# A fused attention and two-layer kernel: batch 0's first keys, second half's masks, their copies and part of a decoding on other engines

## The chip, the core and the metric

The kernel runs on one core of a Trainium2 chip. The metric is the device time of one execution in microseconds. Engines are named as in the profile: PE is TensorE, PEld its weight loads, DVE VectorE, ACT ScalarE, POOL GpSimd, SP SyncE with its DMA queue.

## The reference

Attention with a causal mask and a bias that decays with the positions, then a gated layer, then a second layer; all in fp32.

```python
cum = np.cumsum(np.maximum(s, 0.0), axis=-1)
bias = -(cum[:, :, :, None] - cum[:, :, None, :])
scores = np.where(causal, -1000000000.0, scale * q @ k.T + np.minimum(bias, 0.0))
attn = np.exp(scores - np.max(scores, axis=-1, keepdims=True))
attn = attn / (np.sum(attn, axis=-1, keepdims=True) + 1e-09)
x = attn @ v                       # 4 batches, 8 heads, 576 positions, head size 64
x = (silu(x @ w_gate) * (x @ w_val)) @ w_out      # 2304 x 512, inner size 1536
out = silu(x @ w_in) @ w_out2                     # inner size 2048
```

## The kernel before

Attention goes by batch `b`, head pair `g` and half: half A holds query tiles 0 to 2 (rows 0 to 319), half B tiles 3 and 4 (rows 320 to 575). One such half is a unit; batch 0 has units 0 to 7 (A and B in turn). A unit goes through these functions:

- `masks` (L189): GpSimd writes the row of biases with the causal mask into `e` by `affine_select`. For half A that is the whole row (GATE is 0), for half B only the last 128 columns of each tile; the columns ahead of GATE are read from `c` directly.
- `score_mm` (L203): TensorE makes the scores of both heads side by side, each on 64 rows of the array (the head size is 64).
- `score_min` (L220): VectorE adds scores and biases into `e` and keeps the extreme of each row. Where a piece crosses GATE it is cut in two (one part from `c`, one from `e`).
- `expo` (L240), `inverse` (L250): exponentials and their sums on ScalarE, the inverse of the sums on VectorE.
- `first_keys` (L259) and `normal` (L270): they scale the rows by the inverse. `first_keys` writes the first 64 keys of both heads beside each other into a tile `z` (on ScalarE in half A and in the last unit, on GpSimd else); `normal` scales the other columns in place on GpSimd.
- `turn_mm` (L276): in batch 0 first 8 products of the identity with itself, which nobody reads (fillers); then TensorE transposes 128x128 blocks of `e` and the `z` tiles into PSUM.
- `turned` (L301): copies the two PSUM tiles to `pt`, tile 0 on ScalarE and tile 1 on VectorE.
- `value_mm` (L311): probabilities by values, 64 columns for each head, both side by side; `x_high` and `x_low` split the result into two parts.

For the first 66.5 us (batch 0) all engines run in the order of the code: `first_slot(u)` (L745) issues scores of unit `u`, values of unit `u - 2` and turns of unit `u - 1`; ScalarE's and VectorE's queues have `expo` and `score_min` of `u` ahead of the copies of `u - 1`. Between the slots stand the decoding of weight chunk 0 (`decode`, `unpack` L388: two ScalarE copies out of 64-bit words, then two VectorE operations, in slots 2, 3, 5 and 6) and its cut into two parts (`w_cut`). Behind batch 0 only TensorE's order is written by hand; batches 1 to 3 of the attention are mixed there with the first layer (`gate` L522, `down` L534), and the other engines' order is chosen by a scheduler.

PSUM: batch 0's scores use all four buffers of `ps_m` for each unit, so a unit's scores wait until `score_min` of the unit before has read a bank. Turns and values share two buffers of `ps_a`.

Of the kernel before, what the change touches and what calls it, by code (L numbers as in the profile page):

```python
# [8 lines left out]
F32 = mybir.dt.float32  # L9
F32R = mybir.dt.float32r  # L10
U32 = mybir.dt.uint32
AF = mybir.ActivationFunctionType
ALU = mybir.AluOpType

B, H, S, D = 4, 8, 576, 64
NT, DM = B * S, H * D
F1, F2 = 1536, 2048
P = 128
# [11 lines left out]
TILES = [(0, 64), (64, 128), (192, 128), (320, 128), (448, 128)]  # L30
# [32 lines left out]
QMASK = 1.0e9  # L63
# [3 lines left out]
def kernel(  # L67
# [9 lines left out]
    nc = tc.nc  # L77
# [5 lines left out]
    def pool(name, bufs, space=None, scope=ctx, side="left"):  # L83
        kw = {"space": space} if space is not None else {}
        return scope.enter_context(tc.tile_pool(name=name, bufs=bufs, side=side, reuse_waits="tile", **kw))
# [14 lines left out]
    z_p = pool("z", 4, scope=attention, side="right")  # L100
# [9 lines left out]
    def copy(eng, out, in_, scale=1.0):  # L110
        if eng == "a":
            act_last[:] = [nc.scalar.activation(out=out, in_=in_, func=AF.Copy, scale=scale).ins]  # L112
        elif eng == "v":
            nc.vector.tensor_scalar(out=out, in0=in_, scalar1=scale, scalar2=None, op0=ALU.mult)
        else:
            nc.gpsimd.tensor_scalar(out=out, in0=in_, scalar1=scale, scalar2=1.0, op0=ALU.mult, op1=ALU.mult)


    ident = const.tile([P, P], F32, name="ident")
# [29 lines left out]
    st = {}  # L149
    first_v, first_z = [], []  # L150

    def zeros():
        for n in range(2):
            t = zero_p.tile([P, P], F32, tag=f"v0_{n}", name="vz")
            nc.vector.memset(t, 0.0)
            first_v.append(t)
        first_z.append(zero_p.tile([P, P], F32, tag="z0", name="z0"))
        nc.vector.memset(first_z[0], 0.0)

    def qk_load(b, g):  # L160
        t = qkr_p.tile([P, 2, S], F32, tag="qkr", name="qkr")
        for i in range(2):
            nc.sync.dma_start(out=t[i * D : i * D + D], in_=qk[b, 2 * g + i].rearrange("t d s -> d t s"))
        st[b, g, "qkc"] = (t, None)
# [24 lines left out]
    def masks(b, g, half):  # L189
        c = st[b, g, "qkc"][1]  # L190
        es = st[b, g, half, "e"] = {}
        for i in HALF[half][0]:
            q0, r = TILES[i]
            g0, wd = GATE[i], q0 + r
            e = e_p.tile([P, 2, S], F32, tag="e", name="e")
            for hd in range(2):
                nc.gpsimd.affine_select(
                    out=e[:r, hd, g0:wd], in_=c[:r, hd, g0:wd], pattern=[[-1, wd - g0]], compare_op=ALU.is_ge,
                    fill=-8.0 * QMASK, base=q0 - g0, channel_multiplier=1,
                )  # L200
            es[i] = e

    def score_mm(b, g, half):  # L203
        t = st[b, g, "qkc"][0]
        if b == 0:
            banks = [[ps_m.tile([P, 512], F32, tag="m", name="psc") for _ in range(2)] for _ in range(2)]
        else:
            banks = [ps_a.tile([P, 2, 512], F32, tag="a", name="psc") for _ in range(2)]
            banks = [[p[:, 0], p[:, 1]] for p in banks]
        st[b, g, half, "s"] = banks  # L210
        for i, bank, o, c0, n in PACK[half]:
            q0 = TILES[i][0]
            for hd in range(2):
                d0 = hd * D
                nc.tensor.matmul(  # L215
                    out=banks[bank][hd][:, o : o + n], lhsT=t[d0 : d0 + D, 0, q0 : q0 + P],
                    rhs=t[d0 : d0 + D, 1, c0 : c0 + n], start=True, stop=True,
                )

    def score_min(b, g, half, i):  # L220
        c, e, banks = st[b, g, "qkc"][1], st[b, g, half, "e"][i], st[b, g, half, "s"]
        r, g0 = TILES[i][1], GATE[i]
        m = [None, None]
        for k, bank, o, c0, n in PACK[half]:
            if k != i:
                continue
            for hd in range(2):
                for k0, end, gate in ((c0, min(g0, c0 + n), c), (max(g0, c0), c0 + n, e)):
                    if k0 >= end:
                        continue  # L230
                    m2 = sm_p.tile([P, 1], F32, tag="m", name="m")
                    nc.vector.tensor_tensor_reduce(  # L232
                        out=e[:r, hd, k0:end], in0=banks[bank][hd][:r, o + k0 - c0 : o + end - c0],
                        in1=gate[:r, hd, k0:end], scale=-0.125,
                        scalar=3.0e38 if m[hd] is None else m[hd][:r], op0=ALU.add, op1=ALU.min, accum_out=m2[:r],
                    )
                    m[hd] = m2
        st[b, g, half, "m", i] = m
# [18 lines left out]
        nc.vector.reciprocal(out=rl[:r], in_=l[:r])  # L257

    def first_keys(b, g, half, i):  # L259
        r, e, rl = TILES[i][1], st[b, g, half, "e"][i], st[b, g, half, "l", i]  # L260
        z = first_z[0] if i == 0 else z_p.tile([P, P], F32, tag="z", name="z")
        st[b, g, half, "z", i] = z
        for hd in range(2):
            f = rl[:r, hd : hd + 1]
            if half in ZACT or (b, g) == (0, NP - 1):
                nc.scalar.activation(out=z[:r, hd * D : hd * D + D], in_=e[:r, hd, :D], func=AF.Copy, scale=f)
            else:
                copy("g", z[:r, hd * D : hd * D + D], e[:r, hd, :D], f)

    def normal(b, g, half, i):  # L270
        r, e, rl = TILES[i][1], st[b, g, half, "e"][i], st[b, g, half, "l", i]
        for hd in range(2 if i > 0 else 0):
            x = e[:r, hd, D : sum(TILES[i])]
            copy("g", x, x, rl[:r, hd : hd + 1])

    def turn_mm(b, g, half):  # L276
        tiles, base, n = HALF[half]
        es = st.pop((b, g, half, "e"))
        ps = [ps_a.tile([P, 2, 512], F32, tag="a", name="ptr") for _ in range(2)]
        put = []  # L280
        for _ in range(8 if b == 0 else 0):
            nc.tensor.matmul(out=ps[0][:, 0, :P], lhsT=ident, rhs=ident, start=True, stop=True)
        for j, tile, o in PLACE[half]:
            k0 = TILES[j][0]
            for i in tiles:
                q0, r = TILES[i]
                if q0 < k0:
                    continue
                for hd in range(2):
                    x = o + q0 - max(k0, base)  # L290
                    nc.tensor.transpose(ps[tile][:, hd, x : x + r], es[i][:r, hd, k0 : k0 + P], ident[:r, :r])  # L291
            off = max(k0, base) - base
            put.append((j, tile, o, off, n - off))
        for i, tile, hd, o in PLACE0[half]:
            q0, r = TILES[i]
            z = st.pop((b, g, half, "z", i))
            r = P
            nc.tensor.transpose(ps[tile][:, hd, o : o + r], z[:r], ident[:r, :r])
        st[b, g, half, "p"] = (ps, put, [None, None])

    def turned(b, g, half, k):  # L301
        n = HALF[half][2]
        ps, _, pt = st[b, g, half, "p"]
        pt[k] = pt_p.tile([P, 2, 512], F32, tag="pt", name="pt")
        w = WIDE[half][k]
        if w is None:
            copy("av"[k], pt[k][:, 0, :n], ps[k][:, 0, :n])
        else:
            copy("av"[k], pt[k][:, :, :w], ps[k][:, :, :w])

    def value_mm(b, g, half):  # L311
        tiles, base, n = HALF[half]
# [74 lines left out]

    def unpack(zz, t, k, part="av"):  # L388
        lo, hi = t[:, :, 0], t[:, :, 1]
        if "a" in part:  # L390
            nc.scalar.activation(out=zz, in_=hi.bitcast(F32), func=AF.Copy, scale=2.0**-112)
            nc.scalar.activation(out=k, in_=lo, func=AF.Copy, scale=0.937 * 2.0**-29)
        if "v" in part:
            nc.vector.scalar_tensor_tensor(
                out=k, in0=zz.bitcast(U32), scalar=3, in1=k, op0=ALU.logical_shift_left, op1=ALU.bitwise_or
            )
            nc.vector.scalar_tensor_tensor(
                out=zz.bitcast(U32), in0=hi, scalar=0x80000000, in1=k, op0=ALU.bitwise_and, op1=ALU.bitwise_or
            )
# [345 lines left out]
    def first_slot(u):  # L745
# [37 lines left out]
        if x:  # L783
            if u < H - 1:
                inverse(*x, tiles[-1])
                masks(*units[u + 1])
                first_keys(*x, tiles[-1])
            normal(*x, tiles[-1])
# [10 lines left out]
    def body():  # L799
        everything = ExitStack()  # L800
        everything.enter_context(tc.manual_schedule(engines=None))
        setup()
        zeros()
        qk_load(*pairs[0])
        qk_load(*pairs[1])
# [241 lines left out]
```

## Time and profile before

| what | us |
|---|---|
| median of 3 runs | 1011.53 (1010.31 to 1012.63) |
| span of the profiled execution, first to last instruction (no other time of it is given) | 1010.2 |
| TensorE busy | 999.4 |
| first 66.5 us (batch 0): TensorE busy | 62.68 |
| 66.5 to 105 us: TensorE busy | 36.26 of 38.50 |
| 105 us to the end: TensorE busy | 900.44 of 905.20 |

The profiled execution's span is 1.3 us under the median of the runs. A busy time of TensorE is the time in which a product is in flight; how close the products follow each other is read from the starts of the groups in the timeline.

### The profile page before, as it was taken

How to read it: one execution, taken by the hardware profiler on the slowest of the kernel's cores; microseconds unless marked ns; L12 is line 12 of the kernel's file. 1: busy time of each engine (PE TensorE's matmuls, PEld its weight loads, DVE VectorE, ACT ScalarE, POOL GpSimd, SP SyncE). 2: the span in 40 equal slices, each digit the busy share in tenths (PEclk: the TensorE clock that was granted, in tenths of full speed). 3: DMA queues.
4: the chain of work that ended last, by engine and by line, in shares of the span. 5: the costliest groups of instructions: out<-in, count | busy, mean ns of one | idle time of the engine just before them, and what ended most of it. 6: DMA issues, size and time to landing. Idle time of an engine off the chain costs nothing.

```text
span 1010.2 us, 19666 instructions
## 1 busy us (share of the span) xinstructions
PE 999.4 (99%) x6992; PEld 942.4 (93%) x6992; DVE 565.3 (56%) x1434; ACT 530.0 (52%) x1294; POOL 590.7 (58%) x753
## 2 busy tenths in 40 slices
PE   8999999999999999999999999999999999999998
PEld 6788898899899899988899999999999999999998
DVE  5887847635645645445552323266666566665555
ACT  6878877615665536665542443244544335543333
POOL 4667765613976655756651665455467458674445
PEclk9999999999999999999999999999999999999999
DMA  8688897758797799876668686797767866896662
GB/s 233 160 266 298 268 349 233 258 180 276 244 332 250 254 317 307 284 240 239 254 232 314 243 308 247 287 391 294 263 249 271 321 228 253 292 342 233 243 225 103
DMA packets 81619, 267.19 MB, mean 265 GB/s; under 512 B 9904, under 2 KB 29360, under 8 KB 66160
## 3 DMA queue, kind: packets, MB, share of 16 engines
q1 hardware_dynamic: 81376, 265.73, 75.2%
q8 instruction: 55, 0.90, 0.4%
q14 instruction: 44, 0.36, 0.1%
q10 hardware_dynamic: 144, 0.20, 0.1%
HBM read 208.15 MB, written 57.75 MB: 263 GB/s over the span
## 4 chain that ended last, share of the span: by engine, by line
PE 93%; ACT 2%; DMA 2%; POOL 1%; DVE 1%; issue 1%; SPq 0%; POOLq 0%; DVEq 0%
PE pgv L504 9%; PE pgv L505 9%; PE pgv L506 9%; PE pu L646 6%; PE pu L650 6%; PE pu L649 6%; PE po L691 6%; PE po L692 6%; PE po L693 6%; PE po L504 5%; PE pv L333 5%; PE po L505 5%; PE po L506 5%; PE psc L215 4%; PE ptr L291 3%; DMA r<-in_w_dram 1%
## 5 line engine op out<-in xcount | busy, mean ns | idle before, releaser
L504 PE MATMUL pgv<-xt,wt 128*128 128x288 f32 x768 | 229.5, 299 | 1.2 <-DVE u L515 1.2
L505 PE MATMUL pgv<-xt,wt 128*128 128x288 f32 x768 | 226.3, 295 | 0.1
L506 PE MATMUL pgv<-xt,wt 128*128 128x288 f32 x768 | 226.1, 294 | 0.0
L623 POOL TENSOR_TENSOR h<-u,h 128x384 fp32r<-128x384 f32 x72 | 75.1, 1043 | 142.1 <-ACT h L112 127.9
L504 PEld LDWEIGHTS pgv<-xt,wt 128*128 128x128 f32 x768 | 144.1, 188 | 12.3 <-DVE m L232 6.3
L505 PEld LDWEIGHTS pgv<-xt,wt 128*128 128x128 f32 x768 | 144.1, 188 | 0.3 <-DVE xt L348 0.3
L506 PEld LDWEIGHTS pgv<-xt,wt 128*128 128x128 f32 x768 | 144.0, 188 | 0.0
L112 ACT ACTIVATE h<-u 128x288 fp32r<-128x288 f32 (+1 forms) x168 | 79.8, 475 | 95.4 <-DVE u L516 94.3
L518 POOL TENSOR_TENSOR h<-u,h 128x288 fp32r<-128x288 f32 x96 | 80.0, 836 | 83.1 <-ACT h L112 83.1
L504 PE MATMUL po<-h,wt 128*128 128x288 f32 x384 | 114.8, 299 | 0.0
L505 PE MATMUL po<-h,wt 128*128 128x288 f32 x384 | 113.1, 294 | 0.0
L506 PE MATMUL po<-h,wt 128*128 128x288 f32 x384 | 113.0, 294 | 0.0
L691 PE MATMUL po<-h,wt 128*128 128x384 f32 x336 | 112.4, 335 | 0.0
L692 PE MATMUL po<-h,wt 128*128 128x384 f32 x336 | 112.3, 334 | 0.0
L693 PE MATMUL po<-h,wt 128*128 128x384 f32 x336 | 112.3, 334 | 0.0
L646 PE MATMUL pu<-x,wt 128*128 128x384 f32 x330 | 111.8, 339 | 0.1
L649 PE MATMUL pu<-x,wt 128*128 128x384 f32 x330 | 111.7, 339 | 0.0
L650 PE MATMUL pu<-x,wt 128*128 128x384 f32 x330 | 111.7, 339 | 0.0
L623 POOL TENSOR_TENSOR h<-t,h 128x384 fp32r<-128x384 f32 x96 | 107.2, 1139 | 5.5 <-ACT h L112 5.5
L652 ACT ACTIVATE s<-pu 128x384 f32<-128x384 f32 x48 | 23.6, 492 | 149.6 <-PE pu L650 149.6
L245 ACT ACTIVATE e<-e,m 64x64 f32<-64x64 f32 (+4 forms) x160 | 88.4, 554 | 25.3 <-DVE m L232 24.7
L702 DVE TENSOR_TENSOR acc<-po,acc 128x384 f32<-128x384 f32 x144 | 76.8, 557 | 36.3 <-PE po L693 35.6
(113 smaller groups left out, 2227.8 us busy)
## 6 DMA issues: line engine op xcount, KB each, us to landing
wt<-w_d SPq DMA_DIRECT2D x54, 1024.0 KB, 7.0
wt<-wu_d SPq DMA_DIRECT2D x48, 1024.0 KB, 9.0
wt<-wu_d SPq DMA_DIRECT2D x47, 768.0 KB, 6.5
r<-in_w_dram SPq DMA_DIRECT2D x36, 512.0 KB, 6.7
w_d<-wt SPq DMA_DIRECT2D x18, 1024.0 KB, 8.4
r<-in_w_dram SPq DMA_DIRECT2D x64, 256.0 KB, 7.2
qkr<-in_qk_dram SPq DMA_DIRECT2D x32, 288.0 KB, 8.0
cumb<-cum_d SPq DMA_DIRECT2D x15, 576.0 KB, 9.2
```

Source lines behind the costliest of these rows:

```text
L245: nc.scalar.activation(out=e[:r, hd, :wd], in_=e[:r, hd, :wd], func=AF.Exp, bias=m[hd][:r], scale=-1.0, accum_out=l[:r, hd : hd + 1],)
L504: nc.tensor.matmul(out=ps[:, :n], lhsT=a, rhs=xh, start=(k == 0), stop=False)
L505: nc.tensor.matmul(out=ps[:, :n], lhsT=a, rhs=xl, start=False, stop=False)
L506: nc.tensor.matmul(out=ps[:, :n], lhsT=c, rhs=xh, start=False, stop=(k == last))
L518: engines[LO[ph]].tensor_tensor(out=lo, in0=u, in1=hi.bitcast(F32), op=ALU.subtract)
L623: nc.gpsimd.tensor_tensor(out=h[:, 1], in0=u, in1=h[:, 0].bitcast(F32), op=ALU.subtract)
L646: nc.tensor.matmul(out=o, lhsT=a, rhs=x[:, 0, kk], start=fresh and kk == 0, stop=False, skip_group_check=True)
L649: nc.tensor.matmul(out=o, lhsT=a, rhs=x[:, 1, kk], stop=False, **more)
L650: nc.tensor.matmul(out=o, lhsT=c, rhs=x[:, 0, kk], stop=kk == 1, **more)
L691: nc.tensor.matmul(out=ps, lhsT=a, rhs=h[:, 0], start=fresh, stop=False, skip_group_check=True)
L692: nc.tensor.matmul(out=ps, lhsT=a, rhs=h[:, 1], stop=False, **more)
L693: nc.tensor.matmul(out=ps, lhsT=c, rhs=h[:, 0], stop=e == 1, **more)
```

## The change

All of it acts on batch 0 only, and on the decoding of chunk 0 in slots 2, 3, 5 and 6.

- A tile `tri` is made once: 0 on and under the diagonal, -8e9 above it. In half B `masks` issues nothing; after each pair of score products two products with the identity add the columns of `tri` that fall on the diagonal block to the scores in PSUM. `score_min` then reads the biases from `c` over the whole piece, in one piece.
- `first_keys` issues nothing in batch 0; `normal` scales all columns, also of tile 0. `turn_mm` turns the first 64 keys of each head by a product with the identity into 64 PSUM rows, two products for each tile in place of one transpose of `z`.
- Both `pt` copies of half B are on ScalarE.
- The copy of the high words in `unpack` is on GpSimd where the two parts of the decoding are issued apart (chunk 0); elsewhere it stays on ScalarE.

```diff
+        tri = st["tri"] = z_p.tile([P, P], F32, tag="z", name="tri")
+        nc.gpsimd.affine_select(
+            out=tri, in_=first_z[0], pattern=[[-1, P]], compare_op=ALU.is_ge, fill=-8.0 * QMASK, base=0,
+            channel_multiplier=1,
+        )
...
-            for hd in range(2):
+            for hd in range(0 if b == 0 and half == "B" else 2):
                 nc.gpsimd.affine_select(
...
+            lo, end = max(q0, c0), min(q0 + P, c0 + n)
+            for hd in range(2 if b == 0 and half == "B" else 0):
+                nc.tensor.matmul(
+                    out=banks[bank][hd][:, o + lo - c0 : o + end - c0], lhsT=ident, rhs=st["tri"][:, lo - q0 : end - q0],
+                    start=False, stop=True, skip_group_check=True,
+                )
...
+        if b == 0 and half == "B":
+            g0 = sum(TILES[i])
...
     def first_keys(b, g, half, i):
+        if b == 0:
+            return
...
-        for hd in range(2 if i > 0 else 0):
-            x = e[:r, hd, D : sum(TILES[i])]
+        for hd in range(2 if i > 0 or b == 0 else 0):
+            x = e[:r, hd, D if b > 0 else 0 : sum(TILES[i])]
...
+            if b == 0:
+                for k in range(2):
+                    nc.tensor.matmul(
+                        out=ps[tile][k * D : k * D + D, hd, o : o + r], lhsT=es[i][:r, k, :D], rhs=ident[:r, :r],
+                        start=True, stop=True,
+                    )
+                continue
...
+        eng = "a" if (b, half) == (0, "B") else "av"[k]
...
-            copy("av"[k], pt[k][:, :, :w], ps[k][:, :, :w])
+            copy(eng, pt[k][:, :, :w], ps[k][:, :, :w])
...
+        if part == "a":
+            copy("g", zz, hi.bitcast(F32), 2.0**-112)
+        elif "a" in part:
+            nc.scalar.activation(out=zz, in_=hi.bitcast(F32), func=AF.Copy, scale=2.0**-112)
         if "a" in part:
-            nc.scalar.activation(out=zz, in_=hi.bitcast(F32), func=AF.Copy, scale=2.0**-112)
             nc.scalar.activation(out=k, in_=lo, func=AF.Copy, scale=0.937 * 2.0**-29)
```

TensorE's queue from the scores of unit 1 (half B) to the turns of unit 0, before (`psc` scores, `ptr` turned blocks, `z` first keys; the 128x128 identity products are the fillers):

```order
L215 MATMUL psc<-qkr 128x448 x2
L215 MATMUL psc<-qkr 128x64 x2
L215 MATMUL psc<-qkr 128x512 x2
L282 MATMUL ptr<-ident 128x128 x8
L291 MATMUL ptr<-ident,e 128x128 x6
L298 MATMUL ptr<-ident,z_151 128x128
L298 MATMUL ptr<-ident,z 128x128 x2
```

The same place after the change:

```order
L220 MATMUL psc<-qkr 128x448 x2
L226 MATMUL psc<-tri,ident 128x128 x2
L220 MATMUL psc<-qkr 128x64 x2
L226 MATMUL psc<-tri,ident 128x64 x2
L220 MATMUL psc<-qkr 128x512 x2
L226 MATMUL psc<-tri,ident 128x64 x2
L297 MATMUL ptr<-ident 128x128 x8
L306 MATMUL ptr<-ident,e 128x128 x6
L313 MATMUL ptr<-ident,e 64x64 x2
L313 MATMUL ptr<-ident,e 64x128 x4
```

Six mask products now stand between the score pairs, and six products stand for three transposes; the rest of TensorE's queue is the same in both kernels.

GpSimd's queue from unit 0's last `normal` to the masks of unit 4, before (`e` from `cumb` is a mask, `e` from `e,rl` a `normal`):

```order
L116 TENSOR_SCALAR e<-e,rl 128x256 x2
L116 TENSOR_SCALAR z<-e,rl 128x64 x2
L116 TENSOR_SCALAR e<-e,rl 128x384 x2
L197 AFFINE_SELECT e<-cumb 64x64 x2
L197 AFFINE_SELECT e<-cumb 128x192 x2
L197 AFFINE_SELECT e<-cumb 128x320 x2
L116 TENSOR_SCALAR z<-e,rl 128x64 x2
L116 TENSOR_SCALAR e<-e,rl 128x512 x2
L116 TENSOR_SCALAR e<-e,rl 128x128 x2
L197 AFFINE_SELECT e<-cumb 128x128 x4
L116 TENSOR_SCALAR e<-e,rl 128x256 x2
L116 TENSOR_SCALAR z<-e,rl 128x64 x2
```

The same place after the change:

```order
L116 TENSOR_SCALAR e<-e,rl 128x320 x2
L116 TENSOR_SCALAR e<-e,rl 128x448 x2
L202 AFFINE_SELECT e<-cumb 64x64 x2
L202 AFFINE_SELECT e<-cumb 128x192 x2
L202 AFFINE_SELECT e<-cumb 128x320 x2
L116 TENSOR_SCALAR e<-e,rl 128x576 x2
L116 TENSOR_SCALAR e<-e,rl 64x64 x2
L116 TENSOR_SCALAR e<-e,rl 128x192 x2
L116 TENSOR_SCALAR e<-e,rl 128x320 x2
L116 TENSOR_SCALAR wraw<-r_181 128x512
L116 TENSOR_SCALAR e<-e,rl 128x448 x2
```

The four selects of half B and the `z` products are gone, the `normal` rows are 64 columns wider, and the decode copy of the first quarter of chunk 0 (`wraw`) stands behind unit 2's `normal` and ahead of unit 3's.

ScalarE's queue in slot 2 (half A of unit 2, copies of unit 1), before:

```order
L112 ACTIVATE xt<-pv 128x320
L266 ACTIVATE z_151<-e,rl 64x64 x2
L245 ACTIVATE e,l<-e,m 128x320 x2
L266 ACTIVATE z<-e,rl 128x64 x2
L112 ACTIVATE pt<-ptr 128x1024
L266 ACTIVATE z<-e,rl 128x64 x2
L391 ACTIVATE wraw<-r_177 128x512
L392 ACTIVATE dk<-r_177 128x512
```

The same place after the change:

```order
L112 ACTIVATE xt<-pv 128x320
L258 ACTIVATE e,l<-e,m 128x320 x2
L112 ACTIVATE pt<-ptr 128x1024 x2
L418 ACTIVATE dk<-r_181 128x512
L258 ACTIVATE e,l<-e,m 128x448 x2
```

The `z` products and one decode copy left ScalarE, and the second `pt` copy came. Behind batch 0 the queues of ScalarE, VectorE, GpSimd and SP differ by some swapped rows up to about 100 us of the trace of before, and not behind.

## Rows read from the trace of the kernel before

**Rows 1.** The page, part 1: busy time, share of the span, instructions.
```profile
PE 999.4 (99%) x6992; PEld 942.4 (93%) x6992; DVE 565.3 (56%) x1434; ACT 530.0 (52%) x1294; POOL 590.7 (58%) x753
```
**Rows 2.** Windows: stretch, length, busy us and instructions of each engine, granted clock, DMA.
```profile
0.00:66.50 66.50, 62.68 (x476) 48.35 (x477) 47.86 (x200) 49.08 (x139) 38.40 (x94) 0.97 0.76 206
66.50:105.00 38.50, 36.26 (x277) 32.43 (x276) 31.09 (x86) 32.48 (x78) 27.67 (x40) 1.00 0.89 312
105.00:1010.20 905.20, 900.44 (x6244) 861.67 (x6242) 486.31 (x1149) 448.49 (x1079) 524.59 (x620) 1.00 0.75 267
```
**Rows 3.** TensorE's waits up to 110 us: in total, times, longest, in us.
```profile
PE pv L333 <- ACT pt L112: 1.4, 2, 0.8
...
PE pgv L504 <- DVE u L515: 1.2, 2, 0.7
PE ptr L298 <- DVE m L232: 0.9, 1, 0.9
```
**Rows 4.** Timeline of TensorE, steady part: start, length, line, tiles, shape, records.
```profile
40.10 2.10 PE L215 MATMUL psc<-qkr 64*128 64x448 f32 x12
42.14 1.73 PE L333 MATMUL pv<-pt,vrb 128*64 128x256 f32 x16
43.70 0.61 PE L333 MATMUL pv<-pt,vz 128*64 128x128 f32 x8
44.24 2.05 PE L282 MATMUL ptr<-ident 128*128 128x128 f32 x16
46.13 0.82 PE L291 MATMUL ptr<-ident,e 128*128 128x128 f32 x6
46.78 0.49 PE L298 MATMUL ptr<-ident,z 128*128 128x128 f32 x3
47.20 1.36 PE L215 MATMUL psc<-qkr 64*128 64x64 f32 x12
48.49 0.76 PE L333 MATMUL pv<-pt,vz 128*64 128x320 f32 x4
...
51.72 1.82 PE L291 MATMUL ptr<-ident,e 128*128 128x128 f32 x14
...
53.69 2.10 PE L215 MATMUL psc<-qkr 64*128 64x448 f32 x12
```
**Rows 5.** Timeline of TensorE, units 1 to 4.
```profile
10.29 2.61 PE L215 MATMUL psc<-qkr 64*128 64x448 f32 x12 [0.47 <-DVE m L232]
12.83 2.05 PE L282 MATMUL ptr<-ident 128*128 128x128 f32 x16
...
15.79 1.63 PE L215 MATMUL psc<-qkr 64*128 64x64 f32 x10
...
19.15 1.09 PE L333 MATMUL pv<-pt,vz 128*64 128x320 f32 x4 [0.79 <-ACT pt L112]
...
25.83 2.10 PE L215 MATMUL psc<-qkr 64*128 64x448 f32 x12
...
37.45 0.75 PE L291 MATMUL ptr<-ident,e 128*128 128x128 f32 x3
```
**Rows 6.** Timeline of TensorE from 47.2 us, first and second pair step.
```profile
47.20 0.33 PE L215 MATMUL psc<-qkr 64*128 64x64 f32 x2
...
47.20 0.44 PE L215 MATMUL psc<-qkr 64*128 64x64 f32 x4
```
**Rows 7.** Groups by line and shape, 8 to 66.5 us: busy, mean ns, idle before.
```profile
L112 ACT ACTIVATE pt<-ptr 128x1024 f32<-128x1024 f32 x4 | 4.1, 1026 | 1.7 <-PE ptr L291 1.7
...
L114 DVE TENSOR_SCALAR pt<-ptr 128x1024 f32<-128x1024 f32 x3 | 3.7, 1224 | 2.7 <-PE ptr L298 2.4
...
L116 POOL TENSOR_SCALAR e<-e,rl 128x512 f32<-128x512 f32 x8 | 5.9, 754 | 1.8 <-DVE rl L257 1.8
```
**Rows 8.** Windows of TensorE: busy us and records, granted clock, DMA.
```profile
18.00:19.00 1.00, 0.36 (x2) 1.00 1.13 285
...
20.00:21.00 1.00, 1.00 (x8) 0.50 1.06 208
```

More of the change, by code (lines that the diff above doesn't have):

```diff
@@ L305, in turned @@
         w = WIDE[half][k]
+        eng = "a" if (b, half) == (0, "B") else "av"[k]
         if w is None:
-            copy("av"[k], pt[k][:, 0, :n], ps[k][:, 0, :n])
+            copy(eng, pt[k][:, 0, :n], ps[k][:, 0, :n])
         else:
-            copy("av"[k], pt[k][:, :, :w], ps[k][:, :, :w])
+            copy(eng, pt[k][:, :, :w], ps[k][:, :, :w])
     def value_mm(b, g, half):
```

## The prediction

> **What bounds the kernel now.** I read first the page's line of engine totals and the table of stages. TensorE is busy 99% of the span [rows 1]; after 105 us it has 900.44 us of work in 905.20 [rows 2]. The diff touches only batch 0's attention and chunk 0's decoding, the first 66.5 us, so the question is what paces these. TensorE is busy 62.68 of 66.50 us there, VectorE 47.86, ScalarE 49.08, GpSimd 38.40 [rows 2]. The table of waits then shows how little TensorE waits for anyone in that stretch: 1.4 us for `pt` copies in two waits, and some shares of a microsecond beside them [rows 3]. The timeline of one pair of half units shows groups that follow each other without a hole: scores of half B at 40.10, values, 16 filler steps of `turn_mm`, transposes, scores of half A at 47.20, and so on to 53.69 [rows 4]. The fillers (8 products for each half, 1.89 us) run whether or not anyone is late; the diff keeps all of them. So TensorE's own work paces steady batch 0, and every product that is added there counts in full. Only the first two halves (10 to 26 us) and the transposes at 37.45 show lost time [rows 5]. From 66.5 to 105 us there are waits on VectorE of 1.2 and 0.9 us [rows 3] that the diff does not aim at.
>
> **The price of one step.** An fp32 product is two steps in the records, an fp32 transpose is one. Six transposes take 46.13 to 46.78, 0.11 us each; 16 filler steps take 44.24 to 46.13, that is 16 times 0.112 and 0.10 left over [rows 4]. Products with 64 columns run in pairs side by side: the vz group (8 records, 4 pair steps of 0.11) takes 43.70 to 44.24, again 0.10 more than its steps [rows 4]. So where the array goes from one shape (64-row pairs, 64-column pairs, full) to another, 0.10 us go before the first step and 0.10 after it: 0.20 us a switch. The other end agrees: three transposes from 46.78 leave 0.09 us before 47.20 [rows 4].
> How long is a 64-wide step? In the scores of half A the second 64-wide step ends 0.11 us after the first (0.33, then 0.44) [rows 6], like a 128-wide one, not half of it.
> Beside these rows stand two pages. The Trainium skill, TensorEngine Tiling (Array Packing), Key Properties, says that a change of tiling mode drains TensorE; this speaks against the change, and the 0.10 us gaps above agree. The Trainium skill, TensorE: Matmul & The Clock Gate, LDWEIGHTS, says that a weight load goes by the columns of the stationary operand, 128 over 1.2 or 107 ns, whatever streams after it; by streaming alone the masks of a half would cost 0.4 us less, and the 0.11 of the row sides with the load.
>
> **The change part by part.**
> *Masks by TensorE.* For each of 4 halves B six products with the identity: 12 steps of 0.112 or 1.34 us. They stand between the score pairs, so a half gains five switches (into the full array three times, back to 64-row pairs twice; the last way out replaces the switch that was there): 5 times 0.20 is 1.0. The 64- and 512-wide pairs already wait some 0.1 for their loads, so I take 2.2 us a half, 8.8 in all. Bounds: 1.4 (64-wide steps at half, a switch at 0.10) to 2.4, or 5.6 to 9.6.
> *First keys.* Half A loses three transposes (0.33) and gains three pairs: 4 pair steps of 0.11 and 2 smaller ones of 0.055 to 0.11, a change to 64 columns (0.15), and perhaps one between the 64-row and the 128-row pair: +0.37 to +0.62, taken 0.5. Half B loses two transposes (0.22) and gains two pairs (0.44) and the switch (0.15): +0.37. Eight halves: 3.5 us, bounds 3.0 to 4.0.
> TensorE gains 12.3 us of work.
> *What the other engines lose and gain.* VectorE loses the 1.22 us copy of half B and the reduces that were cut at the diagonal; ScalarE loses the z products and four decode copies and gains the 1.03 us copy for the 1.22 [rows 7]; GpSimd loses half B's selects and its z products, and gains 64 columns in each `normal` and four 128x512 copies, each near the 0.75 us of its 128x512 product [rows 7] (bounds 0.6 to 1.5, since the source has a stride). None of it stands in front of TensorE in the steady part: in half A's slot `pt` tile 0 of half B is complete some 1.1 us before the turns end, so ScalarE's two copies end about 1.1 us after the turns, and the next scores of half B, now 4.2 us, run meanwhile. GpSimd's decode copy stands behind the slot's `normal`; behind it waits the next half's `normal`, due about 5 us later. I set these edits to zero; if that cover were gone, a late copy would cost up to 1 us a pair.
> *What TensorE's waits give back.* Second half's masks no longer wait on GpSimd in unit 1, so VectorE's reduces start as soon as the scores exist. (1) Unit 1's scores take 10.29 to 12.83, 2.54 us where 40.10 to 42.14 takes 2.04: 0.5 lost to late banks [rows 4, 5]. (2) Unit 2's scores and the wait for `pt` take 15.79 to 19.15, 3.36 where 47.20 to 48.49 takes 1.29: 2.07 [rows 4, 5]. In the new order unit 1's scores end near 14.5, the turns of unit 0 near 18.0, unit 2's scores near 19.3; the last reduce of unit 1 ends near 16.1 and its exponentials near 17.1, the copy of unit 0 near 17.9 and the small one on VectorE near 18.6. All are in time, so both losses go: 2.57. (3) 19.15 to 25.83 takes 6.68 where 48.49 to 53.69 takes 5.20 [rows 4, 5]: the granted clock is 0.50 (1.2 GHz) at 20 to 21 us, after a microsecond in which TensorE was busy 0.36 [rows 8]. Without that idle I expect no drop: 1.48. (4) The transposes from 37.45 reach the next scores at 40.10, 2.65 us, where 51.72 to 53.69 takes 1.97 [rows 4, 5]: a wait for `normal` on GpSimd, 0.68, gone since half B's selects and z products leave that queue and TensorE comes later. What stays: the start of unit 1, which waits for unit 0's reduces, and the second `pt` wait (0.6 of rows 3), because VectorE's copy of the last A half still follows the turns. Sum: 4.73.
> *After 66.5 us.* The program's order changes by some swapped rows up to about 100 us and not at all behind. ScalarE now copies `pt` tile 1 of the last half (1.03) ahead of the decoding of chunk 1, and no longer its four z products. Bounds: 2.1 less (both waits of rows 3 go) to 1 more; taken 0.
> *Sum:* 12.3 - 4.73 = +7.5 us on a span of 1010.2. The runs shown have a median of 1011.53, 1.3 above the span; I add to the median: 1019.0.
>
> **The rivals.**
> *The clock drops anyway* (or later): the wait ahead of unit 1's scores stays, and only one drop is there to learn from. Then 1.48 is not given back: 1020.5. Chance 0.14.
> *The masks are cheap:* the 64-wide steps run at half and a switch costs only its gap. 8.8 becomes 5.6: 1015.8. For it: in half B's scores the loads do hide partly. Against it: the 0.11 of rows 6. Chance 0.13.
> *The added copy on ScalarE or the one on GpSimd is late* at the end of batch 0, where the first gate products wait for chunk 0's weights and the decoding of chunk 1 is queued behind the copy: 1 to 2 us more, 1020.5. Chance 0.08.
> *No measurable change:* cheap masks and in addition the waits of 1.2 and 0.9 us behind 66.5 gone: 1015.8 - 2.1 = 1013.7, and a little more such luck is within 0.2%. Chance 0.05.
> *Faster, because VectorE sets the pace:* a score group can hold waits that no row shows as waiting, as unit 2's did. If all of batch 0 were so, TensorE's added products would fill holes and only the 4.73 us would count: 1006.8. It decides from the point where VectorE's work for a pair of halves exceeds TensorE's, 13.59 us from 40.10 to 53.69. VectorE has 47.86 in 66.5, and the groups of rows 4 fit their steps to 0.1 us, so there are no holes. Chance 0.05.
>
> **How the numbers follow.** The forecast itself (1017 to 1021) has 0.55. A measurement of this kernel tells some 0.2% or 2 us from no change. Slower by more: 0.55 + 0.14 + 0.13 + 0.08 = 0.90; within: 0.05; faster: 0.05. The range takes in the forecast, the clock that stays, the late copies and most of the cheap masks, 1015 to 1022; what it leaves out is the two last rivals and the corners, under 2 in 10.
>
> **What would show it.** In the changed kernel's trace: half B's scores with masks, from first score to first value product, take 4.2 us instead of 2.04 (3.4 if masks are cheap); the first-key group takes 0.85 in half A and 0.6 in half B; TensorE's clock is 1.00 from 10 us on; the first gate product starts near 74 instead of 66.5, and from there to the end everything is as long as before. I am wrong if steady half units do not lengthen by 2.2 and 0.4 to 0.5, if new waits of TensorE stand behind ScalarE's copies, or if the part behind the first gate product changes by more than 2 us.

## The result and the profile after

The changed kernel takes 1024.03 us (median of 6 runs, 1023.51 to 1025.42); the kernel before takes 1011.67 beside it. The ratio is 1.0125, 95% interval 1.0113 to 1.0137: slower by 1.25%. The sign and the mechanism in batch 0 were as forecast; the time lies 5 us above the forecast and 2 us outside its range.

The profiled execution of the changed kernel spans 1021.8 us and took 1023.81. Windows of it, cut at the first gate product (`pgv`) and at the first output product (`po`); the part between the two is called the late stretch below. The columns: stretch, length, busy us and records of TensorE, its weight loads, VectorE, ScalarE and GpSimd, granted clock, DMA share, GB/s. They answer [rows 1, 2].

```profile
0.00:74.88 74.88, 72.41 (x584) 55.37 (x584) 42.46 (x165) 43.34 (x110) 38.21 (x81) 1.00 0.66 187
74.88:132.42 57.54, 54.13 (x399) 48.37 (x397) 41.13 (x111) 48.01 (x119) 36.03 (x54) 0.97 0.80 279
132.42:1021.80 889.38, 884.22 (x6121) 847.29 (x6119) 474.88 (x1123) 433.52 (x1038) 513.45 (x604) 1.00 0.75 267
```

The same cut of the kernel before, which the prediction did not make:

```profile
66.50:121.42 54.92, 52.68 (x400) 46.83 (x398) 42.92 (x112) 47.48 (x119) 38.64 (x56) 1.00 0.85 296
121.42:1010.20 888.78, 884.02 (x6121) 847.26 (x6119) 474.48 (x1123) 433.49 (x1038) 513.62 (x604) 1.00 0.75 267
```

The 11.6 us between the spans are 8.38 up to the first gate product (74.88 for 66.50), 2.62 from there to the first output product (57.54 for 54.92), and 0.60 behind it. The first stretch got a full clock (1.00 for the 0.97 of rows 2); in the second the clock fell to a mean of 0.97 where it had been 1.00. VectorE and ScalarE lost 5.4 and 5.7 us of work in batch 0 and TensorE gained 9.7 (72.41 for 62.68).

The steady half units after, TensorE's timeline as in [rows 4] (start, length, line, tiles, shape, records):

```profile
42.23 1.02 PE L220 MATMUL psc<-qkr 64*128 64x448 f32 x4
43.18 0.71 PE L226 MATMUL psc<-tri,ident 128*128 128x128 f32 x4
43.82 0.44 PE L220 MATMUL psc<-qkr 64*128 64x64 f32 x4
44.19 0.66 PE L226 MATMUL psc<-tri,ident 128*128 128x64 f32 x4
44.78 1.13 PE L220 MATMUL psc<-qkr 64*128 64x512 f32 x4
45.84 0.66 PE L226 MATMUL psc<-tri,ident 128*128 128x64 f32 x4
46.42 1.73 PE L356 MATMUL pv<-pt,vrb 128*64 128x256 f32 x16
...
51.16 0.92 PE L313 MATMUL ptr<-ident,e 64*64 64x64 f32 x12
52.01 1.36 PE L220 MATMUL psc<-qkr 64*128 64x64 f32 x12
...
58.15 0.66 PE L313 MATMUL ptr<-ident,e 128*64 128x128 f32 x8
58.74 1.02 PE L220 MATMUL psc<-qkr 64*128 64x448 f32 x4
```

Half B's scores with masks run from 42.23 to 46.42, 4.19 us for 2.04; the first keys take 0.85 in half A (51.16 to 52.01) and 0.59 in half B (58.15 to 58.74). A pair of halves takes 16.51 (42.23 to 58.74) for 13.59.

TensorE's waits up to 120 us (in total, times, longest), as in [rows 3]:

```profile
PE pgv L530 <- DVE wraw L423: 2.6, 1, 2.6
...
PE pv L356 <- ACT pt L112: 0.6, 1, 0.6
PE pgv L531 <- DVE xt L371: 0.6, 1, 0.6
```

Of the waits of [rows 3], one of the two for `pt` is left, and that for `m` is gone. At the top stands a new one, a gate product that waits 2.6 us for VectorE's decoding (L423), 38 us behind the end of batch 0 (112.69 less 74.88). These are the links of that wait, from the timelines of GpSimd, VectorE, ScalarE and TensorE (the bracket tells the idle time before an instruction and what ended it):

```profile
106.26 0.88 POOL L202 TENSOR_SCALAR_AFFINE_SELECT e<-cumb 128x320 f32<-128x320 f32 x2
107.08 0.82 POOL L544 TENSOR_TENSOR h<-u,h 128x288 fp32r<-128x288 f32 x1
```
```profile
107.94 0.45 DVE L541 SCALAR_TENSOR_TENSOR u<-th,pgv 128x288 f32<-128x288 f32 x1 [2.83 <-POOL h L544]
...
110.44 0.69 DVE L420 SCALAR_TENSOR_TENSOR dk<-wraw,dk 128x512 uint32<-128x512 uint32 x1
...
111.96 0.68 DVE L423 SCALAR_TENSOR_TENSOR wraw<-r,dk 128x512 uint32<-128x512 uint32 x1
```
```profile
108.43 0.64 ACT L418 ACTIVATE dk<-r 128x512 uint32<-128x512 uint32 x1 [1.76 <-DVE u L541]
```
```profile
112.69 0.40 PE L530 MATMUL pgv<-xt,wt 128*128 128x288 f32 x1 [2.63 <-DVE wraw L423]
```

Read it from the top. On GpSimd a 320-column select of batch 1's mask stands ahead of `h`. VectorE's `u` waits for that `h` until 107.94, 2.83 us. ScalarE's next decoding of chunk 2 writes `dk` into the PSUM banks (pool `ps_m`) that the gate's `pgv` also uses, and waits until `u` has read its bank: 1.76 us. The decoding on VectorE starts late in turn. Between its second L420 (110.44) and its second L423 (111.96) VectorE also runs another `u` and some reduces. That L423 ends at 112.64; by the bracket it frees what TensorE's next `pgv` waits for, a bank of the shared pool. In the kernel before, GpSimd ran `h` ahead of that select:

```profile
97.56 0.83 POOL L518 TENSOR_TENSOR h<-u,h 128x288 fp32r<-128x288 f32 x1
98.33 1.37 POOL L197 TENSOR_SCALAR_AFFINE_SELECT e<-cumb 128x320 f32<-128x320 f32 x4
```

After the wait TensorE's clock falls. Windows of TensorE (busy us and records, granted clock, DMA):

```profile
111.00:112.00 1.00, 0.00 (x0) 1.00 0.45 188
113.00:114.00 1.00, 1.00 (x8) 0.70 0.33 74
114.00:115.00 1.00, 1.00 (x6) 0.50 0.91 233
...
116.00:117.00 1.00, 1.00 (x7) 0.59 0.24 45
```

### The profile page after: what moved, and what is told of

Its sections match the earlier page's. It is cut to its first block, busy times and chain, and to the rows that moved or that the text cites. A ratio compares the mean times of both kernels' runs of the same rounds, so it can differ in the third digit from the quotient of the medians.

```text
span 1021.8 us, 19781 instructions
## 1 busy us (share of the span) xinstructions
PE 1010.8 (99%) x7100; PEld 951.0 (93%) x7100; DVE 558.5 (55%) x1398; ACT 524.9 (51%) x1266; POOL 587.7 (58%) x738
## 4 chain that ended last, share of the span: by engine, by line
PE 92%; ACT 3%; DVE 2%; DMA 2%; issue 1%; POOL 0%; DVEq 0%; POOLq 0%; SPq 0%; ACTq 0%
PE pgv L530 9%; PE pgv L532 8%; PE pgv L531 8%; PE pu L672 6%; PE pu L676 6%; PE pu L675 6%; PE po L717 6%; PE po L718 6%; PE po L719 6%; PE pv L356 5%; PE po L530 5%; PE po L531 5%; PE po L532 5%; PE psc L220 5%; PE ptr L306 4%; PE ptr L297 2%
## 5 line engine op out<-in xcount | busy, mean ns | idle before, releaser
L116 POOL TENSOR_SCALAR e<-e,rl 128x256 f32<-128x256 f32 (+8 forms) x136 | 73.4, 554 | 62.0 <-DVE rl L270 40.5
```

## The experiments

The theory after the comparison: batch 0 did what was forecast; the rest of the miss is the late wait with its clock drop, and the edit of the `pt` copies alone brings it, because with that edit the planner writes the rows behind batch 0 in another order on ScalarE, VectorE and GpSimd. The rivals: the masks or the first keys move the late rows or cost more than their steps; the late wait is a chance of one execution; the PSUM banks are not its last link.

### Each edit alone, and the copies undone

**The changed kernel without the copies edit (e1).**

```diff
-        eng = "a" if (b, half) == (0, "B") else "av"[k]
+        eng = "av"[k]
```

> The changed kernel with one part undone: the second pt copy of half B is on VectorE again. Theory: batch 0 got longer by TensorE's added products, 8.4 us to the first gate product, and the further 3 us behind it (a 2.6 us wait of TensorE near 110 us on VectorE's decoding of chunk 2, and a clock drop after it) come from the order which the scheduler chose for ScalarE, VectorE and GpSimd once that copy is on ScalarE. Then this kernel has the first gate product where the changed kernel has it (74 to 75 us), no wait over 1 us near 110 us, no clock drop, and takes 1019.5 to 1021.5. Rival: the late wait comes from TensorE reaching that place later, whatever the order: the wait stays, 1023.5 to 1024.5.

Measured: 1021.27 us (1020.73 to 1022.46), ratio 1.0092 (1.0077 to 1.0107), 2.76 less than the whole change. From the first gate product to the first output product it takes 55.04 us instead of 57.54, and no microsecond of it shows a granted clock under 0.95. GpSimd's `h` is ahead of the select again, and the longest late wait is 1.3 us (the theory allowed none over 1). GpSimd's timeline, VectorE's and TensorE's wait:

```profile
105.75 0.81 POOL L544 TENSOR_TENSOR h<-u,h 128x288 fp32r<-128x288 f32 x1
106.51 1.36 POOL L202 TENSOR_SCALAR_AFFINE_SELECT e<-cumb 128x320 f32<-128x320 f32 x4
```
```profile
106.59 0.45 DVE L541 SCALAR_TENSOR_TENSOR u<-th,pgv 128x288 f32<-128x288 f32 x1 [2.03 <-POOL h L544]
...
109.10 0.69 DVE L420 SCALAR_TENSOR_TENSOR dk<-wraw,dk 128x512 uint32<-128x512 uint32 x1
109.82 0.69 DVE L423 SCALAR_TENSOR_TENSOR wraw<-r,dk 128x512 uint32<-128x512 uint32 x1
```
```profile
PE pgv L530 <- DVE u L541: 1.6, 2, 1.3
```

VectorE's `u` waits for `h` here too, 2.03 us instead of 2.83, so the select adds 0.8. And the second L423 follows its L420 at once, where in the changed kernel some 0.8 us of other rows stand between the two.

**The kernel before with the copies edit alone (e2)** (the same `eng` line put into `turned`).

```diff
-            copy("av"[k], pt[k][:, :, :w], ps[k][:, :, :w])
+            copy(eng, pt[k][:, :, :w], ps[k][:, :, :w])
```

> The kernel before with one part of the change alone: both pt copies of half B on ScalarE. Theory: TensorE's work in batch 0 is unchanged, the first gate product comes within 1 us of 66.5, but the late order is the changed kernel's, so TensorE waits 2 to 3 us near 100 us and its clock drops after it: 1014 to 1015.5. Rival (the late wait needs the later TensorE): no such wait, 1011 to 1012.5.

Measured: 1014.88 (1012.60 to 1016.58), ratio 1.0027 (1.0016 to 1.0039), 2.7 us more than before. The select is ahead of `h`, and the wait is there with the same length:

```profile
96.29 0.87 POOL L197 TENSOR_SCALAR_AFFINE_SELECT e<-cumb 128x320 f32<-128x320 f32 x2
97.12 0.81 POOL L533 TENSOR_TENSOR h<-u,h 128x288 fp32r<-128x288 f32 x1
```
```profile
PE pgv L519 <- DVE wraw L412: 2.6, 1, 2.6
```

A clock drop followed from 103 to 107 us (0.73, 0.50, 0.50, 0.56), and the late stretch took 57.97; VectorE's rows stand between L420 and L423 (L409 and L412 there) as in the changed kernel. The first gate product came at 64.48, 2 us before 66.5 and not within 1: the first score started at 7.83, and the early clock drop of the kernel before (19 to 23 us) did not occur. So for the late wait the copies edit is enough, and e1 shows that it is needed. Which of the swapped rows it needs, no run shows, since none swapped one pair alone.

**The masks alone (e3)**, in the kernel before (`tri`, no selects for half B, and the six products of each half).

```diff
+            for hd in range(2 if b == 0 and half == "B" else 0):
+                nc.tensor.matmul(
...
```

> The kernel before with one part alone: half B's masks added by TensorE, none by GpSimd. Theory: four times 2.2 to 2.3 us of TensorE work, less the early waits of units 1, 2 and 4 and the early clock drop (up to 4.7), which stood on GpSimd's selects: first gate product 70.5 to 72, time 1015.5 to 1017.5, late part as in the kernel before. Rival: the masks hide beside other work, the first gate product stays at 66.5 or comes earlier, 1010 to 1012.

Measured: 1016.50 (1015.17 to 1017.35), ratio 1.0042 (1.0027 to 1.0057), +4.3 us. The first gate product starts at 70.93; the late stretch takes 54.23, and the early waits for `pt` are down to one of 0.6.

**The first keys alone (e4)**, in the kernel before (products with the identity in place of the `z` copies and transposes).

```diff
+            if b == 0:
+                for k in range(2):
+                    nc.tensor.matmul(
...
```

> The kernel before with one part alone: first keys turned by products with the identity, z products gone. Theory: 3.5 us of TensorE work over eight half units; the early waits stand on GpSimd's selects of half B and mostly stay: first gate product 69 to 70.5, 1014 to 1015.5. Rival: the z products on ScalarE and GpSimd were what made TensorE wait, so the early waits go with them: first gate product 66 to 67, 1010.5 to 1012.5.

Measured: 1015.29 (1014.08 to 1016.69), ratio 1.0030 (1.0018 to 1.0042), +3.1 us. The first gate product came at 68.38, earlier than expected, in part because the early clock drop did not occur in this execution, although both `pt` waits (1.4 in all) stood there as in [rows 3].

**The decoding alone (e12)**, in the kernel before.

```diff
+        if part == "a":
+            copy("g", zz, hi.bitcast(F32), 2.0**-112)
...
```

> The kernel before with only the decoding edit: chunk 0's scaled copy on GpSimd. Theory: GpSimd has room in batch 0 and the late rows keep their order, so nothing changes: 1011 to 1013, first gate product at 65 to 66.5. Rival (the copies delay GpSimd's normal products, for which TensorE waits at 37 us): two or more waits on GpSimd's e of 0.5 us each and 1013.5 to 1015.

Measured: 1013.34 (1011.94 to 1015.50), ratio 1.0020 (1.0010 to 1.0030), +1.8 us; expected was no change. The late stretch is as in the kernel before (54.23), and the first score to the first gate product takes 58.82 where it took 58.04. The early clock drop is no longer than in the kernel before, it only came later (0.64, 0.50, 0.50, 0.66 from 20 to 24 us), and 43.25 us behind the first score (43.26 before) TensorE has lost nothing yet. There the transposes now wait for GpSimd's `e`:

```profile
52.11 0.51 PE L297 MATMUL ptr<-ident,e 128*128 128x128 f32 x3
52.95 1.42 PE L297 MATMUL ptr<-ident,e 128*128 128x128 f32 x11 [0.34 <-POOL e L116]
```

They take 2.41 to the next scores where [rows 4] has 1.97: 0.44. The last `pt` wait and the last half's transposes lose 0.35 more. That is the rival's mechanism at a smaller size: a second wait for `e`, of 0.34 and not of 0.5. It makes 0.8; where the other microsecond lies, this one profile does not show, and it stays open.

Each against the runs of before beside it, the four single edits cost 4.3, 3.1, 2.7 and 1.8 us; their sum, 11.9, is nearly the 12.4 of the whole. Only the copies edit lengthens the late stretch to some 58 us; with the others alone it takes 54.23 to 55.02. The 55.02 are the first keys' (e4), with a wait for `u` as in e1, 1.3 at the longest: they have a late order of their own.

### The dose of the masks

The changed kernel with every mask product issued twice (e6); the masked scores then carry the mask value twice.

```diff
+                nc.tensor.matmul(
+                    out=banks[bank][hd][:, o + lo - c0 : o + end - c0], lhsT=ident, rhs=st["tri"][:, lo - q0 : end - q0],
+                    start=False, stop=True, skip_group_check=True,
+                )
```

> The changed kernel with every mask product issued twice in a row (the second adds the same mask once more, which leaves the masked scores masked). Theory: each half B gets 12 more steps of 0.112 us and no further switch, 1.3 us, 5.4 us in all, all of it on the path: scores with masks take 5.5 us instead of 4.2, time 1029 to 1030.5. Rival: part of the masks is covered by waits or by loads that run anyway: under 3 us more, 1024 to 1027.

TensorE's timeline, half B:

```profile
43.35 1.02 PE L220 MATMUL psc<-qkr 64*128 64x448 f32 x4
44.30 0.49 PE L226 MATMUL psc<-tri,ident 128*128 128x128 f32 x2
44.62 0.39 PE L230 MATMUL psc<-tri,ident 128*128 128x128 f32 x2
...
48.88 1.30 PE L360 MATMUL pv<-pt,vrb 128*64 128x256 f32 x10
```

The group grew from 4.19 to 5.53 us (43.35 to 48.88): 1.34 for 12 more steps, 0.112 each, as forecast. So of the 2.15 that masks cost a half, 1.34 are the steps and 0.8 the switches. The time, 1027.45 (1026.08 to 1029.40), lies 3.4 above the changed kernel's and below what I expected, but in the profiled execution the first score to the first gate product takes 70.90 for 65.58: 5.32, about four times 1.34. The difference lies elsewhere: in that execution the first score started at 7.77 instead of 9.30, and the part behind the first output product took 888.02 instead of 889.38.

### What varies by itself

**The kernel before, once more (e5).**

> The kernel before once more, for a second profile of it. Theory: the early drop of TensorE's clock (19.3 to 22.5 us in the first profile) and the moment at which TensorE's steps get from 0.213 to 0.11 us at the start differ from execution to execution, since two other kernels with the same early waits showed no early drop; so this profile can lack the drop, and the first scores can stand 0.5 us or more away from 8.46. Rival: both are a fixed part of this kernel and stand where they stood, to 0.1 us.

1012.68, span 1010.9. First score at 8.33 (8.46 in the first profile), the clock drop at the same place (0.59, 0.50, 0.50, 0.71 from 19 to 23 us), first gate product to first output product 54.23. So the rival came nearer, except for the late stretch: it is 0.69 shorter than in the first profile, where the wait for `m` took 0.9 and here 0.3.

The 44 executions of the kernel before that were timed beside these runs show the drop as a mean granted clock: 28 have one under 0.999, as both profiles with the drop do, and 16 do not. Their spans have means of 1010.6 and 1009.5.

**The changed kernel, once more (e9).**

> The changed kernel once more, unchanged, for what varies from execution to execution. Theory: the wait of TensorE on VectorE's decoded chunk (2.6 us) and the drop of the granted clock behind it come again, first gate product to first output product 57 to 58 us; the first score starts anywhere from 7.8 to 9.3 us, since that differs by execution and not by kernel. Rival: the late wait was a chance of the one profiled execution, then 54 to 55.5 us and a mean clock of 1.000; or the first score's 9.30 belongs to the changed kernel, then 9.2 to 9.4 again.

1021.93, span 1019.9. The late wait came again, with the same length to 0.02 us, but the clock stayed at 1.00. TensorE's timeline, and its windows around the wait:

```profile
111.12 0.40 PE L530 MATMUL pgv<-xt,wt 128*128 128x288 f32 x1 [2.65 <-DVE wraw L423]
```
```profile
109.00:110.00 1.00, 0.00 (x0) 1.00 0.57 237
...
112.00:113.00 1.00, 1.00 (x10) 1.00 0.79 188
```

The stretch took 56.13 (first gate product 73.27, first output product 129.40). That parts the 57.54 of the first profile: 1.4 are the clock drop, and 1.2 (56.13 less the 54.92 of before; 1.9 against the 54.23 of e5) are the new wait, net of the waits of [rows 3] that it replaced. The first score started at 7.71, not at 9.30: the start belongs to the execution, not to the kernel. From the first score to the first gate product it is 65.56 against 65.58.

### The bank, and the fillers

**Chunk 2's decoded values in SBUF (e10)**, in the changed kernel. The planner then also moves some late rows, so that this is not the bank alone.

```diff
-        if 1 < c < len(L1):
+        if 2 < c < len(L1):
```

> The changed kernel, but chunk 2's decoded values go through SBUF as chunk 1's do, and no longer through the PSUM banks that the gate's products use (the planner then writes some of ScalarE's, VectorE's and GpSimd's late rows in another order too). Theory (the bank is the last link of the late wait): the 2.6 us wait and the clock drop go, first gate product to first output product 54 to 55.5 us instead of 57.5, 1020.5 to 1022. Rival (the order of the late rows itself costs, whatever the bank): another wait of 2 to 3 us takes its place, 57 us or more, 1023 to 1025.

1022.57 (1020.16 to 1022.77), ratio 1.0104 (1.0083 to 1.0125). The 2.6 us wait is gone and the stretch takes 55.05; another wait, of 1.6 us, takes part of its place:

```profile
PE ptr L320 <- DVE m L245: 1.6, 1, 1.6
```

But GpSimd's `h` stands ahead of the select again there (105.04 and 105.81), and VectorE's two decodings follow each other, so the first links are gone as well: this run does not test the bank. That the bank is the last link rests on the bracket and on the pool that both uses share. The time is just above the theory's numbers and cannot tell 1 us.

**The same in the kernel before (e11)** (line 410 there).

> The same edit made in the kernel before. Theory: there TensorE waits only 1.2 us in that stretch for VectorE's u, and no decoding is late, so it gains 0 to 1 us: 1010.5 to 1012.5, first gate product to first output product 53.5 to 55. Rival (any edit that lets the planner write the late rows anew costs 2 to 3 us): 1013.5 to 1015.5.

1013.56 (1011.45 to 1014.71), ratio 1.0018 (1.0007 to 1.0029), at the foot of the rival's numbers. The wait for `u` fell to 0.7, but GpSimd's `e` is now waited for 1.4 in all (0.3 before) and VectorE's `rl` 1.0, and the stretch takes 55.88. A second order of the same rows, and again it costs 1.0 us against the first profile and 1.7 against e5's.

**No fillers**, in the kernel before (e8) and in the changed kernel (e7): the 8 products that `turn_mm` issues in each half of batch 0 are left out.

```diff
-        for _ in range(8 if b == 0 else 0):
+        for _ in range(0 if b == 0 else 0):
```

> The kernel before without the fillers. Theory: here the chain over GpSimd's selects, z products and VectorE's copy is close to TensorE's work (VectorE was busy some 12 of 13.6 us a pair), so waits take most of the fillers' place: first gate product 62 to 66 instead of 66.5 and clock drops, 1008 to 1013. Rival: the fillers were pure loss, 997 to 1003.

> The changed kernel without the 8 filler products of each half unit in batch 0 (the output does not use them). Theory: TensorE's work is what paces batch 0; without fillers it has 15 us less, and since VectorE, ScalarE and GpSimd have less to do than before, most of it shows: first gate product 62 to 68 instead of 74.9, some new waits for normal and pt, perhaps clock drops, 1012 to 1018. Rival: the other engines' chain is as long as TensorE's own work was, so waits take the fillers' place and the clock drops: 1021 to 1026.

The kernel before: 1012.92 (1010.48 to 1015.68), ratio 1.0006 (0.9996 to 1.0016): 15 us of TensorE's steps taken out and nothing gained. Waits took their place:

```profile
PE ptr L291 <- POOL e L116: 8.0, 9, 2.1
PE ptr L298 <- DVE xt L348: 3.1, 3, 1.1
```

From 17 to 27 us the clock was at 0.50 too, but the waits alone fill the place: two of its runs had a mean clock of 0.998, as the kernel before has, and they took 1012.21 and 1012.85.

The changed kernel: 1027.04 (1019.41 to 1029.38), ratio 1.0134 (1.0092 to 1.0176), which cannot be told from the 1.0125 with the fillers, and above both the theory's and the rival's numbers; waits for `e` and `xt` make 4.8 and 3.5, and from 55 to 68 us the clock stood at 0.50. The shortest of its runs, 1019.41, had a mean granted clock of 0.998, the other three 0.988 to 0.992; on the word of this one run, the clock decides there. So the fillers hide waits that are there anyway, and they keep the clock. None of the kernels tried was faster than the one before.

## Why the prediction was wrong

**Masks: right.** 8.8 forecast; four times 2.15 (4.19 less 2.04), 8.6, measured. The rival of cheap masks fell: e6 priced the step at 0.112, though two thirds of the mask products are 64 wide. The Trainium skill, TensorE: Matmul & The Clock Gate, LDWEIGHTS, lets a weight load go by its columns, 107 ns for 128; the 0.112 agrees.

**First keys: right, a little high.** Forecast 3.5. The pair of halves grew by 2.92 (16.51 less 13.59), of which 2.15 are masks; 0.77 a pair, 3.1 in all.

**Waits given back: nearly right.** TensorE's timeline, units 1 to 3, beside [rows 5]:

```profile
11.12 1.26 PE L220 MATMUL psc<-qkr 64*128 64x448 f32 x4 [0.47 <-DVE m L245]
...
15.47 2.00 PE L297 MATMUL ptr<-ident 128*128 128x128 f32 x16
...
18.91 1.36 PE L220 MATMUL psc<-qkr 64*128 64x64 f32 x12
...
20.19 0.76 PE L356 MATMUL pv<-pt,vz 128*64 128x320 f32 x4
...
25.63 1.02 PE L220 MATMUL psc<-qkr 64*128 64x448 f32 x4
```

Unit 1's scores take 4.35, 0.16 more than the steady 4.19: 0.34 of the 0.5 came back. Unit 2's take 1.28 to their values, so the 2.07 went whole. 20.19 to 25.63 takes 5.44 for 6.68; no clock drop. All in all 8.6 + 3.1 less the 7.54 by which batch 0 grew (8.38 less 0.84 of later start) leaves 4.16 given back, for 4.73. The 7.57 of the sum (12.3 less 4.73) is met to 0.03, by luck: two errors of half a microsecond cancel. One thing I took as caused was a chance in part: the early drop was missing in e2, e4 and e11 with the same `pt` waits in place. From the first score to the first gate product the kernel before takes 58.04 and e11, whose batch 0 has the same code, 57.17, so an execution of before without the drop would have seen batch 0 grow by 8.4. And the 1.48 of item (3) was not all clock: without the drop the same stretch still takes 5.80 in e11 (19.92 to 25.72) for the steady 5.20, because the transposes then wait 0.34 for GpSimd's `e` and take 2.57 to the next scores instead of 1.97. The drop had hidden that wait, and the change took both away.

**After 66.5 us: the step that failed.** I took 0 for it, with bounds of -2.1 and +1. The late stretch measured +2.62 in the first profile, 1.2 of it the new wait and 1.4 the clock drop behind it; against the second profile of the kernel before it is +3.31. So the last of the prediction's own signs of being wrong came true: the part behind the first gate product changed by more than 2 us. The working named ScalarE's copy ahead of the decoding of chunk 1, and the swapped rows up to about 100 us, but priced the copy alone. What costs are the swapped rows that the copies edit brings (e1, e2): on GpSimd one select ahead of `h`, for which VectorE, ScalarE and TensorE wait one after another, and on VectorE `u` and reduces ahead of the second decoding. Each delays its next link by 0.8; how the 2.6 us divide between them stays open. No row of before priced another order of these engines, and the bound above should have been the longest chain through the swapped rows, with a clock drop on top, not the one copy. The rival of late copies had the right edit with a wrong place: its 1 to 2 us were to fall at the end of batch 0. The decoding copy, zero in the sum as well, cost 1.8 by itself (e12); in the changed kernel no wait for `e` shows, and batch 0 came out as summed.

**The rest of the 5.0 us.** On spans, 1017.7 was forecast and 1021.8 came. Of these 4.1 us, 2.62 are the late stretch and 0.84 the start, which is chance (e9); 0.60 lie behind the first output product, a part that takes 888.78 and 890.26 in two profiles of the kernel before, and so tells nothing. The last 0.9 is what stands around the span: I added the 1.3 between the median and the one span shown; the changed kernel's profiled execution took 2.0 more than its span, and the median lies 0.2 above that. Why six runs out of six lie at 1023.5 or above while e9 took 1021.93 is settled only as far as that one had no drop and an early start: all six have a mean granted clock of 0.998, as the profile with the drop, and e9 has 0.999.

**The other rivals.** VectorE as the pace: no, TensorE's steps count in full (e6). But the sentence that TensorE's own work paces batch 0 needs a limit, as e8 shows: taking TensorE's steps away gains nothing, because the other engines' chain is as long.

## What to carry to other kernels

When an edit changes the engine of an instruction and a planner sets the order, compare the order of every engine to the end of the difference, and ask of each swapped pair who waits for the one that is now second; "some rows swap" is a risk with a price, not a zero. Here a select of 0.88 us and some 0.8 us of VectorE's rows, each ahead of a row that others waited for, became a wait of 2.6 us through two engines' queues and one shared PSUM pool. An engine that is busy all the time can still be no lever: here added steps cost their full price, while leaving out the fillers gained nothing.

## What the chip showed that was not expected

The first steps of TensorE change speed at a moment that differs from one execution to the next, while the granted clock reads 1.00 throughout. Windows of the changed kernel in its two profiles (busy us and records), the first of them from the execution with the first score at 9.30, the second from that with 7.71:

```profile
4.00:5.00 1.00, 1.00 (x7) 1.00 1.04 242
```
```profile
4.00:5.00 1.00, 1.00 (x10) 1.00 1.05 230
```

The first 24 products take 5.49 us in the one execution and 4.29 in the other. Over the profiles of this study the first score starts between 7.71 and 9.30 us. The clock drop is a chance too: an idle stretch of 2.6 us was followed by one (0.50, 1.2 GHz) in the changed kernel, in e2, e6 and e7, and by none in e9; of e6's four runs two have a mean granted clock of 0.998 and two of 1.000. That late drop cost 1.4 us (57.54 for 56.13). The early one cost less, 0.9 (58.04 for the 57.17 of e11), since a wait for GpSimd takes part of its place; the means of the 44 executions differ by 1.1.
